# An even/odd split of the D-axis DFT, and gate/up weights loaded in small early pieces, in a fused spectral-mixer and gated-MLP kernel

## The chip, the cores and the metric

One core of one Trainium2 chip. The metric is device microseconds of one execution; lower is better. All executions quoted are "fast" (granted TensorE clock close to 1.0 unless said). Names used below: PE is TensorE, PEld its weight loads, DVE VectorE, ACT ScalarE, POOL GpSimd, SP the engine whose queue issues all DMAs. "Span" is the time between the first and the last instruction of the profiled execution; the device time is some 2 us longer.

## The reference, cut to what matters

```python
# x: (1, 2048, 640) bf16;  w_r, w_i: (2048, 321);  w_gate, w_up: (640, 1536);  w_down: (1536, 640)
def reference(x, w_r, w_i, B_x, w_gate, w_up, w_down):
    xn = _layernorm(x, axis=-1)
    X = rfft2(xn.astype(float32), axes=(-2, -1))          # S axis: 2048, D axis: 640
    y = irfft2(X * (w_r + 1j * w_i), s=(2048, 640), axes=(-2, -1)).astype(bfloat16)
    h = (xn @ w_gate) * (xn @ w_up)                        # no activation
    return x + y + h @ w_down
```

## The kernel before

All tensors live in one SBUF arena. The 2048 rows are worked in 16 blocks of 128. Each block goes through LayerNorm (DVE, POOL), a transpose T0 on PE (five 128x128 matmuls) into X^T, the D-axis DFT "D" (PE, against a cosine/sine table `fd`), its eviction, and the first part of the S-axis DFT "S128" (four 128x324 matmuls). After the last block come the middle stages (T1, S16, weight product, T2, S16i), in eleven groups, then the inverse transforms and the down projection. Independently of the spectral chain, 96 "GU" tiles (ten 128x256 matmuls each: gate and up of one 128-feature tile for 256 rows) need only X^T and the weights; each is evicted by ACT and multiplied on DVE or POOL.

The program writes tasks with assumed durations, priorities and dependences; a list scheduler in Python, run when the program is built, fixes the order of every engine's queue. On the chip each queue runs strictly in that order, with semaphore waits. GU tasks have a low priority: they fill PE where the plan finds a gap. "Filler" matmuls on zeros, and a "warm-up" of 56 such matmuls, occupy PE early on where the plan has nothing useful.

```python
# --- D stage of block b (cuts marked ...) ---
def em_t0(c, ...):
    for j in range(5):
        ins = c.e.transpose(psb[...], v_xn[:, sl, j * 128:(j + 1) * 128], v_sm[:, 0, :])
...
def em_d(c, b=b):                                  # 10 matmuls 128x324: 5 chunks of d, real and imaginary
    for j in range(5):
        for cc in range(2):
            ins = c.e.matmul(ps[:, bk + cc, 0:_LP], v_xt[:, j, b * 128:(b + 1) * 128],
                             v_fd[:, j, cc, :], start=(j == 0), stop=(j == 4))
def em_ed(c, ...):                                 # one ACT (or DVE) copy of 2 x 324
    return c.e.activation(v_a[:, ar, :, :], ps[:, bk:bk + 2, 0:_LP], _ACTF.Copy)
...
# --- gate/up weights: 8 slots; tiles 0-3 and 4-7 in two DMAs each of 640 KB, 8-11 later into freed slots ---
_NGW = 8
_FT_GROUPS = ((0, 1, 2, 3, 4, 5, 6, 7), (8, 9, 10, 11))
pl_ = 0.027 if q4 == 0 else 0.047                  # DMA priority; first S128 table has 0.025
...
# --- a GU tile ---
for w in range(2):
    for j in range(5):
        ins = c.e.matmul(ps[:, bk, w * 256:(w + 1) * 256], v_gw[:, w, j, r, :],
                         v_xt[:, j, c8 * 256:(c8 + 1) * 256], start=(j == 0), stop=(j == 4))
...
self.slack = {"pe": 1000.0, "act": 300.0, "dve": 400.0, "pool": 100.0, "sp": 0.0}   # of the planner
```

## Time and profile before

253.41 us, median of 5 runs (252.97 to 255.22); span 251.6 us, granted clock 1.000.

The page's first part gives the busy time of each engine, the second the busy tenths in 40 slices of the span (6.3 us each), the fourth the chain of work that ended last:

```profile
...
PE 244.7 (97%) x2286; PEld 202.2 (80%) x2286; DVE 153.9 (61%) x408; ACT 109.7 (44%) x194; POOL 24.3 (10%) x35
...
PE   8969999999999999999999999999999999999995
...
DVE  5868984208799999984722222222257767766654
...
PE 86%; DVE 5%; DMA 4%; SPq 1%; POOL 1%; issue 1%; ACT 1%
...
```

PE is busy nearly everywhere, and it is 86% of the chain. In windows (us from the start; busy us, with the number of instructions that ran in the window, wholly or in part; then clock and DMA):

```profile
...
core 0: us, PE busy (x) PEld busy (x) DVE busy (x) ACT busy (x) POOL busy (x), PEclk, DMA share, GB/s
...
15.00:60.00 45.00, 44.12 (x407) 34.08 (x405) 26.65 (x83) 25.02 (x40) 21.82 (x29) 1.00 0.52 168
60.00:123.00 63.00, 62.60 (x705) 56.31 (x703) 54.24 (x132) 36.30 (x56) 0.00 (x0) 1.00 0.15 52
123.00:178.00 55.00, 55.00 (x506) 49.11 (x504) 16.49 (x55) 30.12 (x51) 0.00 (x0) 1.00 0.14 31
178.00:240.00 62.00, 62.00 (x471) 45.92 (x470) 40.47 (x87) 12.74 (x36) 0.00 (x0) 1.00 0.23 65
...
```

From 60 us on PE has no gap worth naming (62.60 of 63, 55.00 of 55, 62.00 of 62). DVE is loaded in 15–123 us and less so later. "PE busy" includes the pipelined tail of each matmul and useless filler matmuls, so the page alone doesn't say how much of PE's time is work. The groups that the change touches (line, engine, operation, output and input, count; busy us, mean ns of one; idle time before):

```profile
...
L1019 PE MATMUL ps<-arena 128*128 128x256 bf16 x960 | 108.5, 273 | 2.2 <-DMA arena<-in_B_w_up_dram 2.0 <-ACT arena L1030 0.2
...
L821 PE MATMUL ps<-arena 128*128 128x324 bf16 x160 | 23.8, 300 | 0.4 <-DVE arena L808 0.4
...
L832 ACT ACTIVATE arena<-ps 128x648 bf16<-128x648 f32 x16 | 11.4, 710 | 11.3 <-PE ps L821 11.3
...
```

The mean of 300 ns for a D matmul is the length of its record, from its start to a modelled end. What it costs PE is the step from one start to the next, which the timeline gives (start, us, engine, line, count, idle time before and who ended it):

```profile
...
9.76 0.44 PE L796 MATMUL ps<-arena 128*128 128x128 bf16 x5
...
14.56 1.25 PE L1019 MATMUL ps<-arena 128*128 128x256 bf16 x10 [1.97 <-DMA arena<-in_B_w_up_dram]
...
40.19 2.94 PE L821 MATMUL ps<-arena 128*128 128x324 bf16 x20 [0.39 <-DVE arena L808]
42.97 0.30 PE L842 MATMUL ps<-arena 128*128 128x324 bf16 x1
...
43.52 0.72 PE L796 MATMUL ps<-arena 128*128 128x128 bf16 x10
44.08 0.30 PE L842 MATMUL ps<-arena 128*128 128x324 bf16 x1
...
44.63 2.93 PE L821 MATMUL ps<-arena 128*128 128x324 bf16 x20
...
```

L796 is T0, L821 D, L842 to L845 S128, L1019 GU. Twenty D matmuls, two blocks of them, take 40.19 to 42.97, which is 0.139 us each. The whole round of two blocks, from 40.19 to 44.63, is D, S128 and T0 without a GU tile between. The first GU tile starts at 14.56, after a wait of 1.97 us for the w_up weights.

### The profile page before, as it was taken

Reading aid. Unit: us, or ns where it says so; the run is one execution under the profiler, and the core shown is the slowest. Engines: PE = TensorE matmul, PEld = TensorE weight load, DVE = VectorE, ACT = ScalarE, POOL = GpSimd, SP = SyncE. Lnnn points to the kernel's source line nnn. Section 1 sums busy time; section 2 is a strip of 40 time slices with the busy share of each in tenths; the row PEclk is TensorE's granted clock in tenths of the full one; section 3 lists DMA queues with packets and bytes.
Section 4 is the critical chain, followed back from the end, with each engine's and each line's share of the span. In section 5 each row is a group of like instructions: output and inputs, shape, how many; then the busy total and the mean of one; then the engine's idle time right before and its main releaser. Section 6 shows DMA issues by size and latency. Waiting matters only on the chain.

```text
span 251.6 us, 5511 instructions
## 1 busy us (share of the span) xinstructions
PE 244.7 (97%) x2286; PEld 202.2 (80%) x2286; DVE 153.9 (61%) x408; ACT 109.7 (44%) x194; POOL 24.3 (10%) x35
## 2 busy tenths in 40 slices
PE   8969999999999999999999999999999999999995
PEld 8767766789999999898888888888777777777773
DVE  5868984208799999984722222222257767766654
ACT  2345555664554555557655555555213113113120
POOL 0066978000000000000000000000000000000000
PEclk9999999999999999999999999999999999999999
DMA  6997009328000000107202700000022132122121
GB/s 204 376 387 271 0 9 311 100 55 361 3 0 3 4 0 3 52 3 252 90 26 58 154 3 0 3 0 3 13 63 70 52 85 76 52 81 78 54 79 40
DMA packets 22505, 21.84 MB, mean 87 GB/s; under 512 B 6352, under 2 KB 21072, under 8 KB 22352
## 3 DMA queue, kind: packets, MB, share of 16 engines
q1 hardware_dynamic: 22480, 21.49, 27.4%
q8 instruction: 18, 0.29, 0.5%
q14 instruction: 7, 0.06, 0.1%
HBM read 18.86 MB, written 2.62 MB: 85 GB/s over the span
## 4 chain that ended last, share of the span: by engine, by line
PE 86%; DVE 5%; DMA 4%; SPq 1%; POOL 1%; issue 1%; ACT 1%
PE ps L1019 41%; PE ps L1152 21%; PE ps L821 4%; DMA arena<-in_B_w_up_dram 4%; PE ps L1112 3%; PE ps L1110 3%; PE ps L1067 2%; PE ps L940 2%; PE ps L961 2%; PE ps L884 2%; PE ps L905 2%; PE ps L1077 2%; SPq L647 1%; PE ps L796 1%; POOL arena L784 1%; DVE arena L808 1%
## 5 line engine op out<-in xcount | busy, mean ns | idle before, releaser
L1019 PE MATMUL ps<-arena 128*128 128x256 bf16 x960 | 108.5, 273 | 2.2 <-DMA arena<-in_B_w_up_dram 2.0
L1019 PEld LDWEIGHTS ps<-arena 128*128 128x128 bf16 x960 | 92.8, 98 | 13.4 <-issue 2.1
L1030 ACT ACTIVATE arena<-ps 128x512 bf16<-128x512 f32 x96 | 57.3, 597 | 49.4 <-PE ps L1019 48.8
L1037 DVE TENSOR_TENSOR arena<-arena 128x256 bf16<-128x256 bf16 x93 | 26.9, 289 | 48.4 <-ACT arena L1030 47.9
L1152 PE MATMUL ps<-arena 128*128 128x320 bf16 x384 | 54.6, 299 | 0.0
L1152 PEld LDWEIGHTS ps<-arena 128*128 128x128 bf16 x384 | 37.5, 98 | 13.9
L1121 ACT ACTIVATE arena<-ps 128x321 f32<-128x321 f32 x16 | 7.0, 439 | 52.8 <-PE ps L1112 52.7
L919 DVE TENSOR_TENSOR arena<-ps,arena 128x512 bf16<-128x512 f32 (+1 forms) x44 | 25.3, 636 | 0.0
L821 PE MATMUL ps<-arena 128*128 128x324 bf16 x160 | 23.8, 300 | 0.4 <-DVE arena L808 0.4
L1162 DVE TENSOR_TENSOR arena<-ps,arena 128x320 bf16<-128x320 f32 x32 | 15.6, 488 | 12.5 <-PE ps L1152 12.5
L821 PEld LDWEIGHTS ps<-arena 128*128 128x128 bf16 x160 | 15.2, 97 | 7.2 <-DVE arena L808 0.7
L832 ACT ACTIVATE arena<-ps 128x648 bf16<-128x648 f32 x16 | 11.4, 710 | 11.3 <-PE ps L821 11.3
L972 ACT ACTIVATE arena<-ps 128x1024 bf16<-128x1024 f32 x10 | 10.2, 1022 | 8.8 <-PE ps L961 8.8
L1140 DVE TENSOR_TENSOR arena<-arena 128x640 f32<-128x640 f32 x16 | 13.1, 821 | 1.1
L1112 PE MATMUL ps<-arena 128*128 128x319 bf16 x48 | 13.6, 300 | 0.0
L1110 PE MATMUL ps<-arena 128*128 128x321 bf16 x48 | 13.5, 299 | 0.0
L854 ACT ACTIVATE arena<-ps 128x648 bf16<-128x648 f32 x16 | 11.3, 708 | 4.7 <-PE ps L845 4.7
L773 POOL TENSOR_SCALAR arena<-arena 128x640 bf16<-128x640 bf16 x14 | 11.1, 799 | 14.8 <-DVE arena L718 14.8
L1088 DVE CAST arena<-ps 128x512 bf16<-128x512 f32 x11 | 7.6, 692 | 7.8 <-PE ps L1067 7.8
L808 DVE COPY arena<-ps 128x640 bf16<-128x640 bf16 x16 | 7.3, 480 | 8.0 <-PE ps L796 7.9
L784 POOL TENSOR_SCALAR arena<-arena 128x640 bf16<-128x640 bf16 x14 | 11.0, 796 | 2.2 <-DVE arena L762 1.9
L701 DVE BATCH_NORM_STATS2 arena<-arena 128x6 f32<-128x320 bf16 x16 | 7.6, 475 | 3.7 <-DMA arena<-in_A_x_dram 3.7
(65 smaller groups left out, 227.4 us busy)
## 6 DMA issues: line engine op xcount, KB each, us to landing
arena<-in_A_x_dram SPq DMA_DIRECT2D x18, 160.0 KB, 2.3
out_dram<-arena SPq DMA_DIRECT2D x32, 80.0 KB, 1.9
arena<-c_tinv SPq DMA_DIRECT2D x1, 2048.0 KB, 7.7
arena<-in_A_x_dram SPq DMA_DIRECT2D x3, 640.0 KB, 11.8
arena<-in_B_w_down_dram SPq DMA_DIRECT2D x1, 1920.0 KB, 7.9
arena<-c_t SPq DMA_DIRECT2D x4, 384.0 KB, 10.2
arena<-in_A_w_r_dram SPq DMA_DIRECT2D x1, 1284.0 KB, 7.7
arena<-in_A_w_i_dram SPq DMA_DIRECT2D x1, 1284.0 KB, 11.4
```

The costliest lines, as they stand in the source:

```text
L784: return c.e.tensor_scalar(v_xn[:, sl, :], v_xn[:, sl, :], v_rs[:, b:b + 1], 0.0, AluOpType.mult, AluOpType.add)
L821: ins = c.e.matmul(ps[:, bk + cc, 0:_LP], v_xt[:, j, b * 128:(b + 1) * 128], v_fd[:, j, cc, :], start=(j == 0), stop=(j == 4))
L832: return c.e.activation(dst, src, _ACTF.Copy)
L919: ins = c.e.tensor_tensor(dst, x5[:, :, cc, :, :], wv, AluOpType.mult)
L1019: ins = c.e.matmul(ps[:, bk, w * 256:(w + 1) * 256], v_gw[:, w, j, r, :], v_xt[:, j, c8 * 256:(c8 + 1) * 256], start=(j == 0), stop=(j == 4))
L1030: return c.e.activation(v_gbf[:, rr, :], ps[:, bk, :], _ACTF.Copy)
L1037: return c.e.tensor_tensor(v_ht[:, ft, c8 * 256:(c8 + 1) * 256], v_gbf[:, rr, 0:256], v_gbf[:, rr, 256:512], AluOpType.mult)
L1110: c.e.matmul(ps[:, bk, 0:321], v_z2[:, r3, lt, 0, :], v_g[:, lt, 0:321], start=(lt == 0), stop=(lt == 2))
L1112: ins = c.e.matmul(ps[:, bk + 1, 1:320], v_z2[:, r3, lt, 1, :], v_g[:, lt, 321:640], start=(lt == 0), stop=(lt == 2))
L1140: return c.e.tensor_tensor(v_yn[:, r2, :], v_yn[:, r2, :], v_xr[:, r2, :], AluOpType.add)
L1152: ins = c.e.matmul(ps[:, bk, 0:320], v_ht[:, ft, sa * 128:(sa + 1) * 128], v_wd[:, ft, hf * 320:(hf + 1) * 320], start=(ft == 0), stop=(ft ...
L1162: return c.e.tensor_tensor(v_out[:, r2, sl3], ps[:, bk, 0:320], v_yn[:, r2, sl3], AluOpType.add)
```

## The change

Intent: the cosine of frequency 320 - l at row d is (-1)^d times that of frequency l, and the sine is -(-1)^d times it. So the sums over even d, E(l), and over odd d, O(l), for l = 0 to 160 give all 321 frequencies: X(l) = E(l) + O(l), and X(320 - l) has the real part E - O and the imaginary part O - E. Each half needs 162 columns instead of 324, so D takes 6 matmuls of 324 columns instead of 10 (the d rows are permuted by strided T0 reads into even and odd chunks; the chunk that holds both enters both sums). The price is in the eviction: E + O, E - O and O - E have to be formed, with mirrored writes. Because X^T is now permuted, the gate/up weight rows must be loaded in the same permutation. These loads are also split into 30 DMAs of 128 KB, get 12 resident slots, and the first ten are put ahead of the first S128 table.

```diff
-_NGW = 8
+_NGW = 12
+_DT = ((0, 2), (256, 2), (512, 1), (1, 2), (257, 2))
...
-                    for j in range(5):
-                        for cc in range(2):
-                            ins = c.e.matmul(ps[:, bk + cc, 0:_LP], v_xt[:, j, b * 128:(b + 1) * 128],
-                                             v_fd[:, j, cc, :], start=(j == 0), stop=(j == 4))
+                    for q in range(6):
+                        tj = (0, 1, 2, 2, 3, 4)[q]
+                        ins = c.e.matmul(ps[:, bk + q // 3, 0:324], v_xt[:, tj, b * 128:(b + 1) * 128],
+                                         v_fd[:, q, :], start=(q % 3 == 0), stop=(q % 3 == 2))
...
+                def em_eo(c, td=td, ar=ar):                      # O: PSUM -> SBUF, f32, 324 elements (ACT)
+                    ...
+                    return c.e.activation(v_osb[:, ar, :, :], src, _ACTF.Copy)
                 def em_ed(c, td=td, ar=ar):
-                    src = ps[:, bk:bk + 2, 0:_LP]
-                    ...return c.e.activation(dst, src, _ACTF.Copy)
+                    e3 = ps[:, bk, 0:324].rearrange("p (c l) -> p c l", c=2)
+                    c.e.tensor_tensor(v_a[:, ar, :, 0:161], e3[:, :, 0:161], v_osb[:, ar, :, 0:161], AluOpType.add)
+                    c.e.tensor_tensor(v_a[:, ar, 0, 320:160:-1], e3[:, 0, 0:160], v_osb[:, ar, 0, 0:160],
+                                      AluOpType.subtract)
+                    return c.e.tensor_tensor(v_a[:, ar, 1, 320:160:-1], v_osb[:, ar, 1, 0:160], e3[:, 1, 0:160],
+                                             AluOpType.subtract)
...
-                    pl_ = 0.027 if q4 == 0 else 0.047
+                    if ftp == 0:
+                        pl_ = opts.get("pgw0", 0.022) if q4 == 0 else opts.get("pgw1", 0.032)
+                    else:
+                        pl_ = opts.get("pgw2", 0.07)
+                    for w_, src_ in ((0, B_w_gate), (1, B_w_up)):
+                        for j in range(5):
+                            s0, st = _DT[j]
+                            ...
+                            dma("ld_gw%d_%d_%d" % (f0, w_, j), dst_, src_[s0:s0 + 128 * st:st, fs], 128 * 1024, ...)
```

More of the change, by code (lines that the diff above doesn't have):

```diff
@@ L389, in _bf16_bits, with _dperm @@
     return r.astype(np.uint16)
+_DT = ((0, 2), (256, 2), (512, 1), (1, 2), (257, 2))
+def _dperm():
+    return [np.arange(128, dtype=np.int64) * st + s0 for (s0, st) in _DT]
 def _build_tables():
@@ L415, in _build_tables @@
     t["sm"] = _bf16_bits(sm)
-    d = np.arange(_D, dtype=np.int64)[:, None]
-    l = np.arange(_LP, dtype=np.int64)[None, :]
-    ang = two_pi * ((d * l) % _D).astype(np.float64) / _D
-    valid = (np.arange(_LP) <= 320).astype(np.float64)[None, :]
-    fd = np.zeros((_D, 2, _LP), np.float64)
-    fd[:, 0, :] = np.cos(ang) * valid
-    fd[:, 1, :] = -np.sin(ang) * valid
-    t["fd"] = _bf16_bits(fd.reshape(5, 128, 2, _LP).transpose(1, 0, 2, 3))
+    dmap = _dperm()
+    lv = np.arange(162, dtype=np.int64)[None, :]
+    lval = (np.arange(162) <= 160).astype(np.float64)[None, :]
+    fd = np.zeros((128, 6, 2, 162), np.float64)
+    for q, (tj, par) in enumerate(((0, 0), (1, 0), (2, 0), (2, 1), (3, 1), (4, 1))):
+        dd = dmap[tj][:, None]
+        ang = two_pi * ((dd * lv) % _D).astype(np.float64) / _D
+        sel = ((dmap[tj] % 2) == par).astype(np.float64)[:, None] * lval
+        fd[:, q, 0, :] = np.cos(ang) * sel
+        fd[:, q, 1, :] = -np.sin(ang) * sel
+    t["fd"] = _bf16_bits(fd)
     s1 = np.arange(128, dtype=np.int64)[:, None]
@@ L530, in _build @@
         b_gw = alloc("GW", _NGW * 2 * 5 * 128)
+        b_gwj = [[sch.buf("GW_%d_%d" % (w_, j_), lay["GW"][0] + (w_ * 5 + j_) * _NGW * 128, _NGW * 128)
+                  for j_ in range(5)] for w_ in range(2)]
         b_gbf = alloc("GBF", 3 * 512)
@@ L542, in _build @@
         b_dum = alloc("DUM", 256)
+        b_osb = alloc("OSB", 2 * 648)
         total = cur[0]
@@ L553, in _build @@
         o_at = lay["AT"][0]
-        b_fd = alloc("FD", 5 * 2 * _LP, at=o_at)
-        b_t128 = alloc("T128", 16 * 3 * 128, at=o_at + 5 * 2 * _LP)
+        b_fd = alloc("FD", 6 * 2 * 162, at=o_at)
+        b_t128 = alloc("T128", 16 * 3 * 128, at=o_at + 6 * 2 * 162)
         b_tinv = alloc("TINV", 16 * 2 * 256, at=o_at)
@@ L597, in _build @@
         v_xn = V("XN").rearrange("p (r d) -> p r d", r=_NSLOT_XN)
-        v_fd = V("FD").rearrange("p (j c l) -> p j c l", j=5, c=2)
+        v_fd = V("FD").rearrange("p (q n) -> p q n", q=6)
         v_t128 = V("T128").rearrange("p (s m k) -> p s m k", s=16, m=3)
@@ L602, in _build @@
         v_a = V("A").rearrange("p (r c l) -> p r c l", r=2, c=2)
+        v_osb = V("OSB").bitcast(_F32).rearrange("p (r c l) -> p r c l", r=2, c=2)
         v_yeo = V("YEO").bitcast(_F32).rearrange("p (r n) -> p r n", r=2)
@@ L651, in _build @@
         ld_sm = dma("ld_sm", v_sm, d_sm, 128 * 768, [(b_sm, None)], prio=0.005)
-        ld_fd = dma("ld_fd", v_fd, d_fd, 128 * 6480, [(b_fd, None)], prio=0.015)
+        ld_fd = dma("ld_fd", V("FD"), d_fd.rearrange("p q c l -> p (q c l)"), 128 * 6 * 648, [(b_fd, None)],
+                    prio=0.015)
         ld_t = []
@@ L684, in _build, with em_apad @@
               bank="pair", cls="warm", selffree=True)
+        def em_apad(c):
+            return c.e.memset(v_a[:, :, :, _NL:_LP], 0.0)
+        T("a_pad", ("dve",), 80.0, em_apad, writes=[(b_a, ("pad", 0, 1))], prio=0.5)
         def em_wpad(c):
@@ L795, in em_t0 @@
                     for j in range(5):
+                        s0, st = _DT[j]
                         ins = c.e.transpose(psb[:, bk * 1024 + j * 128: bk * 1024 + (j + 1) * 128],
-                                            v_xn[:, sl, j * 128:(j + 1) * 128], v_sm[:, 0, :])
+                                            v_xn[:, sl, s0:s0 + 128 * st:st], v_sm[:, 0, :])
                     return ins
@@ L823, in em_d @@
                     return ins
-                td = T("D_%d" % b, "pe", 10 * _d_pe_mm(_LP), em_d,
+                td = T("D_%d" % b, "pe", 6 * _d_pe_mm(324), em_d,
                        reads=[(b_xt, ("s", b * 128, (b + 1) * 128)), (b_fd, None)], prio=pb, bank="pair", cls="a")
+                def em_eo(c, td=td, ar=ar):
+                    bk = bank_of(td)
+                    src = ps[:, bk + 1, 0:324].rearrange("p (c l) -> p c l", c=2)
+                    if c.e is nc.scalar:
+                        return c.e.activation(v_osb[:, ar, :, :], src, _ACTF.Copy)
+                    return c.e.tensor_copy(v_osb[:, ar, :, :], src)
@@ L827, in em_ed @@
+                eo = T("eO_%d" % b, _EV32, {"dve": _d_dve_psum(324), "act": _d_act(324)}, em_eo,
+                       writes=[(b_osb, ("r", ar, ar + 1))], prio=pb - 0.001, after=[td])
+                td.deps |= set(d for d in eo.deps if d is not td)
                 def em_ed(c, td=td, ar=ar):
                     bk = bank_of(td)
-                    src = ps[:, bk:bk + 2, 0:_LP]
-                    dst = v_a[:, ar, :, :]
-                    if c.e is nc.scalar:
-                        return c.e.activation(dst, src, _ACTF.Copy)
@@ L833, in em_ed @@
-                    return c.e.tensor_copy(dst, src)
-                ed = T("eD_%d" % b, _EV32, {"dve": _d_dve_psum(2 * _LP), "act": _d_act(2 * _LP)}, em_ed,
-                       writes=[(b_a, ("r", ar, ar + 1))], prio=pb - 0.001, frees=td)
-                td.deps |= set(d for d in ed.deps if d is not td)
+                    e3 = ps[:, bk, 0:324].rearrange("p (c l) -> p c l", c=2)
+                    c.e.tensor_tensor(v_a[:, ar, :, 0:161], e3[:, :, 0:161], v_osb[:, ar, :, 0:161], AluOpType.add)
@@ new lines, in em_ed @@
+                    c.e.tensor_tensor(v_a[:, ar, 0, 320:160:-1], e3[:, 0, 0:160], v_osb[:, ar, 0, 0:160],
+                                      AluOpType.subtract)
+                    return c.e.tensor_tensor(v_a[:, ar, 1, 320:160:-1], v_osb[:, ar, 1, 0:160], e3[:, 1, 0:160],
+                                             AluOpType.subtract)
+                ed = T("eD_%d" % b, "dve", _d_dve_psum(322) + 2 * _d_dve_psum(160), em_ed,
+                       reads=[(b_osb, ("r", ar, ar + 1))], writes=[(b_a, ("r", ar, ar + 1))], prio=pb - 0.001,
+                       frees=td)
@@ L838, in em_s @@
+                td.deps |= set(d for d in ed.deps if d is not td and d is not eo)
                 def em_s(c, b=b, ar=ar):
@@ L983, in _build @@
         for ftp, ftg in enumerate(_FT_GROUPS):
-            if ftp == 0 and opts.get("gw_chunk", 4) == 4:
+            if True:
                 for q4 in range(len(ftg) // 4):
@@ L988, in _build @@
                     fs = slice(f0 * 128, (f0 + 4) * 128)
-                    pl_ = 0.027 if q4 == 0 else 0.047
-                    for w_, src_ in ((0, wgv), (1, wuv)):
-                        dst_ = v_gw[:, w_, :, r0:r0 + 4, :].rearrange("p j r f -> p j (r f)")
-                        dma("ld_gw%d_%d" % (f0, w_), dst_, src_[:, :, fs], 640 * 1024,
-                            [(b_gw, ("r", 8 * w_ + r0, 8 * w_ + r0 + 4))], prio=pl_ + 0.0001 * w_,
-                            semkey=("gw", r0, w_))
+                    if ftp == 0:
[4 more added lines that the diff above has]
+                        for j in range(5):
+                            s0, st = _DT[j]
+                            dst_ = v_gw[:, w_, j, r0:r0 + 4, :].rearrange("p r f -> p (r f)")
+                            dma("ld_gw%d_%d_%d" % (f0, w_, j), dst_, src_[s0:s0 + 128 * st:st, fs], 128 * 1024,
+                                [(b_gwj[w_][j], ("r", r0, r0 + 4))], prio=pl_ + 0.0001 * w_ + 0.00001 * j,
+                                semkey=("gw", r0, w_))
             else:
@@ L1002, in _build @@
                         pl_ = 30.0 + 0.5 * ft
-                    for w_, src_ in ((0, wgv), (1, wuv)):
-                        dma("ld_gw%d_%d" % (ft, w_), v_gw[:, w_, :, r0, :], src_[:, :, fs], 640 * 256,
-                            [(b_gw, ("r", 8 * w_ + r0, 8 * w_ + r0 + 1))], prio=pl_ + 0.0001 * w_,
-                            semkey=("gw2", r0, w_))
+                    for w_, src_ in ((0, B_w_gate), (1, B_w_up)):
+                        for j in range(5):
+                            s0, st = _DT[j]
+                            dma("ld_gw%d_%d_%d" % (ft, w_, j), v_gw[:, w_, j, r0, :],
+                                src_[s0:s0 + 128 * st:st, fs], 128 * 256,
+                                [(b_gwj[w_][j], ("r", r0, r0 + 1))],
+                                prio=pl_ + 0.0001 * w_ + 0.00001 * j, semkey=("gw2", r0, w_))
             for c8 in range(8):
@@ L1022, in _build @@
                     gu = T("GU_%d_%d" % (ft, c8), "pe", 10 * _d_pe_mm(256), em_gu,
-                           reads=[(b_gw, ("r", r, r + 1)), (b_gw, ("r", 8 + r, 8 + r + 1)),
+                           reads=[(b_gwj[w_][j_], ("r", r, r + 1)) for w_ in range(2) for j_ in range(5)] + [
                                   (b_xt, ("s", c8 * 256, (c8 + 1) * 256))],
```

## The prediction

> **What bounds the kernel now.** The page gives PE 97% busy, the chain 86% PE, granted clock 1.000. From 55 us on PE never waits: the windows view shows it busy 55.76 of 56.0 us in 55–111, 55.00 of 55.0 in 123–178, 70.97 of 71.0 in 178–249. Steps between matmuls, from the timeline: 0.109 us for gate/up (128x256), 0.139 for the D-axis DFT (128x324; ten in 1.39 us). At such steps all useful matmuls add up to about 235 of the 251.6 us span. The rest is the tail after PE's last matmul (2.6 us), start-up before the first gate/up matmul at 14.56 us (3.9 us of it useful; the rest warm-up, fillers and a 1.97 us wait for the w_up DMA), and small gaps. Between 26 and 52 us PE runs only T0, D and S128, nearly without gaps: 4.4 us per two blocks, 2.77 of them D. So D is on the bound.
>
> **What changes.**
> 1. D falls from 10 to 6 matmuls per block: 64 x 0.139 = 8.9 us less PE work. The Trainium skill ("TensorE: Matmul & The Clock Gate", Back-to-back issue gap) gives N/2.4 + 2.5 ns, 137.5 for 324; the trace's 139 agrees.
> 2. D's eviction, one ACT copy of 648 elements (710 ns), becomes one ACT copy of 324 (about 440, like the 128x321 copy) and three VectorE operations: 322 elements (about 490, like FIN 128x320) and twice 160 (about 310, between the 128x64 at 214 and the 128x512 at 678). That is 1.1 us per block, 15–18 us more DVE work in the first 55 us, where DVE is now busy 34. The chain from D to S128 lengthens from 0.7 to about 1.7 us.
> 3. Gate/up weights come in 30 DMAs of 128 KB, the first ten ahead of the first S128 table; fd shrinks. Before the first gate/up matmul 2.5 MB must land instead of 3.2: about 2 us earlier, though ten issues at 0.47 us use most of that rate up. The tiles 8–11 lose their 256-byte rows; their reload was hidden, so that gains nothing.
>
> **How much lies on the path.** After 55 us all is PE-bound, with gate/up work left until 178 us, so PE time saved early is filled with gate/up matmuls and comes off the end almost 1:1, if PE is kept fed before 55 us. Ideal: 251.6 - 8.9 - 2 = 240.7 span, 242.5 us time. Against it: the first phase turns DVE-bound (about 50 us of DVE work, plus gate/up products, in some 52 us); queues run in a fixed planned order, and the plan takes the eviction for 0.86 us where I expect 1.1. So PE will wait 2–4 us in 15–58 us. The tail stays.
>
> **Predicted: 244.8 us, range 241 to 249.5.** Faster by over 2%: 0.80; within 2%: 0.18; slower: 0.02.
>
> **What would show it.** 96 D matmuls at the same step; first gate/up matmul at 11–13 us; DVE over 85% busy in 15–55 us, about 168–172 us in total; gate/up matmuls in 26–52 us, where there are none now; new PE waits on DVE (S128 on the butterfly, T0 on LayerNorm), 2–4 us; later phases unchanged in shape; ACT total down about 4 us.
>
> **What would make it wrong.** Faster: the order absorbs the DVE work and PE hardly waits. Slower: the butterfly runs longer than estimated (reversed writes, or waiting for POOL's LayerNorm operations: the tiny tensor_tensor takes 0.7 us beside POOL at 30–38 us), so the D stage ends well after 58 us with PE waiting; or the 128 KB issues delay the x tiles.

## The result, and the profile after

243.98 us, median of 9 runs (243.59 to 245.7), against 253.43 us for the kernel before, median of 16. The ratio is 0.9635, with a 95% interval of 0.9613 to 0.9656. Ratios here and below divide the mean time of one kernel's fast runs by that of the other's of the same rounds on the same chip, so they are not quite the ratio of the quoted medians. The profiled run has a span of 242.9 us and a clock of 1.000.

The page of the kernel after, the lines that answer to those of before:

```profile
...
PE 237.6 (98%) x2242; PEld 198.5 (82%) x2242; DVE 162.1 (67%) x454; ACT 107.5 (44%) x197; POOL 24.3 (10%) x35
...
PE   8989999999999999999999999999999999999995
...
DVE  5877998864579999999737222222377677667654
...
PE 88%; SPq 6%; DMA 3%; DVE 1%; issue 1%; ACT 0%
...
```

The windows of the kernel after:

```profile
...
15.00:60.00 45.00, 44.70 (x406) 36.29 (x404) 36.74 (x136) 29.50 (x55) 23.09 (x30) 1.00 0.54 173
60.00:123.00 63.00, 62.76 (x727) 57.22 (x726) 53.84 (x129) 34.45 (x51) 0.00 (x0) 1.00 0.15 46
...
178.00:240.00 62.00, 62.00 (x470) 45.77 (x467) 41.52 (x91) 12.64 (x36) 0.00 (x0) 1.00 0.24 69
...
```

In 15–60 us DVE went from 26.65 to 36.74 us busy, while PE is as full as before (44.70 us against 44.12). The groups of the kernel after:

```profile
...
L1059 PE MATMUL ps<-arena 128*128 128x256 bf16 x960 | 110.5, 273 | 0.2 <-ACT arena L1070 0.2
...
L841 PE MATMUL ps<-arena 128*128 128x324 bf16 x96 | 15.6, 300 | 0.0
...
L860 DVE TENSOR_TENSOR arena<-ps,arena 128x322 bf16<-128x322 f32 x16 | 7.8, 484 | 3.5 <-ACT arena L851 3.5
...
L851 ACT ACTIVATE arena<-ps 128x324 f32<-128x324 f32 x16 | 7.0, 440 | 3.5 <-PE ps L841 2.4
...
L861 DVE TENSOR_TENSOR arena<-ps,arena 128x160 bf16<-128x160 f32 x16 | 5.1, 316 | 0.0
...
L863 DVE TENSOR_TENSOR arena<-arena,ps 128x160 bf16<-128x160 f32 x16 | 5.0, 312 | 0.0
...
```

D has 96 matmuls instead of 160. The three butterfly operations take 484 + 316 + 312 ns, 1.11 us a block. The PE timeline of the kernel after (L816 is T0, L841 D, L874 to L877 S128, L1059 GU):

```profile
...
12.35 0.44 PE L816 MATMUL ps<-arena 128*128 128x128 bf16 x5
13.72 0.31 PE L874 MATMUL ps<-arena 128*128 128x324 bf16 x1 [0.92 <-DMA arena<-c_t]
...
15.56 2.35 PE L1059 MATMUL ps<-arena 128*128 128x256 bf16 x20
...
42.69 1.26 PE L1059 MATMUL ps<-arena 128*128 128x256 bf16 x10
43.78 0.99 PE L841 MATMUL ps<-arena 128*128 128x324 bf16 x6
44.61 0.30 PE L874 MATMUL ps<-arena 128*128 128x324 bf16 x1
...
45.16 0.99 PE L841 MATMUL ps<-arena 128*128 128x324 bf16 x6
46.00 1.25 PE L1059 MATMUL ps<-arena 128*128 128x256 bf16 x10
...
```

Two things stand out. GU tiles now stand between the D matmuls (42.69, 46.00). And the first GU tile begins at 15.56 us, an S128 having waited 0.92 us for its table: later than before, not earlier.

An account of PE's time makes this exact. Add up, over the whole timeline of PE, the step from each start to the next, by kind of matmul; a wait is then counted with the matmul before it. Totals in us, from the first matmul (1.05 us in both):

```
                           before    after   difference
D                           22.18    13.32     -8.86
warm-up and fillers         10.96    10.63     -0.33
T0                           4.99     5.55     +0.56   (0.92 of after is the wait for the S128 table)
S128                         9.40     8.85     -0.55
GU                         104.88   105.38     +0.50
all other matmuls           95.51    95.45     -0.06
sum                        247.92   239.18     -8.74
```

The span fell by 8.7 us (251.6 to 242.9), the D steps by 8.86. Apart from that, PE's time hardly changed in sum. The tail is the same: the span less 1.05 us less the sum leaves 2.6 us in both.

One part of this sum is chance. The 56 warm-up matmuls, which the change doesn't touch, took 5.78 us in this execution of after and 4.57 in that of before. In both they start about every 107 ns at first and about every 56 ns later, but the slow steps number 52 in after and 28 in before. Over the twelve profiles with 56 warm-up matmuls they took 4.40 to 5.95 us. So 1.2 us of the difference between two profiles at the start need not come from the change, and the profiled run of after (244.8 us) is slower than its median: the two later profiles of the same kernel have spans of 241.9 and 241.6 us.

Yet the D stage itself did not become shorter: the last S128 matmul starts at 53.9 us before and at 60.4 us after. It became longer by 6.5 us while the kernel became shorter by 8.7. In 15–60 us 87 GU matmuls ran before and 190 after.

### The profile page after: what moved, and what is told of

It is laid out like the page before. It is cut to its first block, busy times and chain, and to the rows that moved or that the text cites. A ratio compares the mean times of both kernels' runs of the same rounds, so it can differ in the third digit from the quotient of the medians.

```text
span 242.9 us, 5472 instructions
## 1 busy us (share of the span) xinstructions
PE 237.6 (98%) x2242; PEld 198.5 (82%) x2242; DVE 162.1 (67%) x454; ACT 107.5 (44%) x197; POOL 24.3 (10%) x35
## 4 chain that ended last, share of the span: by engine, by line
PE 88%; SPq 6%; DMA 3%; DVE 1%; issue 1%; ACT 0%
PE ps L1059 41%; PE ps L1192 21%; SPq L661 6%; PE ps L841 4%; DMA arena<-in_A_x_dram 3%; PE ps L1152 3%; PE ps L1150 3%; PE ps L1107 3%; PE ps L972 2%; PE ps L993 2%; PE ps L937 2%; PE ps L916 2%; PE ps L1117 2%; PE ps L816 1%; PE ps L874 1%; PE ps L875 1%
## 5 line engine op out<-in xcount | busy, mean ns | idle before, releaser
L1059 PE MATMUL ps<-arena 128*128 128x256 bf16 x960 | 110.5, 273 | 0.2 <-ACT arena L1070 0.2
L1059 PEld LDWEIGHTS ps<-arena 128*128 128x128 bf16 x960 | 92.7, 98 | 11.7 <-ACT arena L1070 0.4
L1192 PEld LDWEIGHTS ps<-arena 128*128 128x128 bf16 x384 | 37.5, 98 | 13.9
L841 PE MATMUL ps<-arena 128*128 128x324 bf16 x96 | 15.6, 300 | 0.0
L886 ACT ACTIVATE arena<-ps 128x648 bf16<-128x648 f32 x16 | 11.4, 710 | 5.5 <-PE ps L877 5.0
L841 PEld LDWEIGHTS ps<-arena 128*128 128x128 bf16 x96 | 9.2, 97 | 3.6
L860 DVE TENSOR_TENSOR arena<-ps,arena 128x322 bf16<-128x322 f32 x16 | 7.8, 484 | 3.5 <-ACT arena L851 3.5
L1172 DVE TENSOR_TENSOR arena<-arena 128x319 f32<-128x319 f32 x16 | 7.7, 482 | 3.2 <-ACT arena L1162 3.2
L1107 PE MATMUL ps<-arena 128*128 128x256 bf16 x64 | 9.6, 272 | 0.0
```

The source lines that it names most:

```text
L841: ins = c.e.matmul(ps[:, bk + q // 3, 0:324], v_xt[:, tj, b * 128:(b + 1) * 128], v_fd[:, q, :], start=(q % 3 == 0), stop=(q % 3 == 2))
L1107: ins = c.e.matmul(ps[:, bk, lt * 256:(lt + 1) * 256], v_z1[:, sa, cc, 128 * lt:128 * lt + 128], v_tinv[:, sa, cc, :], start=(cc == 0), st ...
L1192: ins = c.e.matmul(ps[:, bk, 0:320], v_ht[:, ft, sa * 128:(sa + 1) * 128], v_wd[:, ft, hf * 320:(hf + 1) * 320], start=(ft == 0), stop=(ft ...
```

## The experiments

Theory A: PE is the bound from 15 us to the end, so the D matmuls removed come off one for one, and GU tiles use the PE time that the slower eviction leaves open. Rivals: B, that the new loads bring part of the gain and the butterfly takes as much back; C, that DVE is now at its limit and PE has time to spare before 60 us; E, that the D stage simply became shorter.

### dft_only and loads_only: each half of the change alone

```diff
# dft_only, against after: loads as before
-_NGW = 12
+_NGW = 8
-   pl_ = opts.get("pgw0", 0.022) ...          # ten DMAs of 128 KB per four tiles, all early
+   pl_ = 0.027 if q4 == 0 else 0.047          # three DMAs per matrix and chunk (rows are permuted), tiles 8-11 late
# loads_only, against before: D stage untouched
-_NGW = 8
+_NGW = 12
+_DT = ((0, 1), (128, 1), (256, 1), (384, 1), (512, 1))   # then the load loop of after
```

> The change with the even/odd D stage alone: gate/up weights ordered, sized and reloaded as before (8 slots, first chunk behind the first S128 table, tiles 8-11 in small DMAs late; each load in three DMAs instead of one because the rows are permuted). Theory A (the gain is the 64 D matmuls taken off PE, the loads add nothing): 243.5 to 244.8 us, as the whole change. Theory B (the early, resident weights bring the roughly 2 us that I predicted, and the DVE butterfly takes about as much back): 245.5 to 247 us.

> The kernel before with the new weight loads alone (12 slots, 30 DMAs of 128 KB, first ten ahead of the first S128 table), D stage untouched. Theory A: 253 to 254.2 us, the same as before within 0.3%. Theory B: 251 to 252 us. Either way the first gate/up matmul should come earlier than 14.56 us.

Measured on one chip, with the kernel before at 253.57 us: dft_only 245.03 us (244.88 to 245.2), ratio 0.9656 (0.9628 to 0.9685); loads_only 251.93 us (251.84 to 252.24), ratio 0.9930 (0.9901 to 0.9959).

So the even/odd DFT alone brings 8.5 us of the gain. Its 245.03 us lies between the ranges of A (to 244.8) and B (from 245.5); its ratio is that of the whole change, as A has it. But the loads alone are worth 1.6 us on the old DFT, 0.4 to 1% by the ratio's interval, where A expected nothing; there B was right. On top of the DFT what they add is not resolved: the whole change had ratios of 0.9635, 0.9652 and 0.9669 in three sets of runs, dft_only 0.9656 in one. The gain of the loads doesn't come the way I had thought either. In loads_only the first GU tile starts at 15.04 us, later than the 14.56 of before, where it had been expected earlier: the 1.97 us wait for w_up is gone, but S128 now waits 1.85 us for its table. By the account of PE's steps, warm-up, fillers, T0 and S128 together shrank by 1.2 us (25.35 to 24.14); of this the fillers, 56 instead of 66, and the wait counted with them are 1.1 us, and T0 is 0.5. What set these free was not tested.

### mm_pad: put the PE time back

```diff
+                    for q in (0, 1, 2, 3):      # overwritten by the real matmuls that follow
+                        c.e.matmul(ps[:, bk + q // 2, 0:324], v_xt[:, q, b * 128:(b + 1) * 128],
+                                   v_fd[:, q, :], start=True, stop=True)
                     for q in range(6):
```

> The changed kernel with four useless 128x324 matmuls put back in front of each D stage (overwritten by the real ones), all queue orders unchanged. Theory A (PE time counts one for one): 64 x 0.139 = 8.9 us more, 252.5 to 253.3 us, about the time before. Rival C (in 15-60 us DVE is the limit and PE has spare time there): less than 4 us more, below 248 us.

Measured: 252.3 us (251.77 to 252.72), ratio 0.9936 (0.9892 to 0.9979). That is about 8 us above the changed kernel's medians (243.98, 244.13 and 244.38 in three other sets of runs), or 6.8 to 7.6 us by the ratios. In its trace the useless matmuls occupy 8.88 us of PE. Most of that comes back, if not quite all that A expected (252.5 us or more). The queues were not replanned, and DVE's work was as heavy as in after. Rival C (less than 4 us) fails: PE has at most 1 to 2 us to spare before 60 us.

### bfly_plus1 and bfly_x2: how much slack DVE has

Each butterfly operation's copy writes to a place that is unused at that time. The order of all queues is the same as in after.

```diff
# bfly_plus1: the third operation twice;  bfly_x2: all three twice
+                    d3_ = v_ht[:, b, 1506:1666] if b < 12 else v_ht[:, b - 4, 1666:1826]
+                    c.e.tensor_tensor(d3_, v_osb[:, ar, 1, 0:160], e3[:, 1, 0:160], AluOpType.subtract)
```

> The changed kernel with the third butterfly operation done twice (the copy goes to an unused place), all queue orders unchanged: 16 x about 0.23 us = 3.7 us more DVE work in 9-59 us. Theory A (DVE has slack behind the gate/up matmuls): 0 to 1.5 us more. Rival C (DVE is at the limit): about 3.7 us more, 247.5 us.

> The changed kernel with all three butterfly operations done twice (copies to an unused place), all queue orders unchanged: 16 x about 0.87 us = 14 us more DVE work before 60 us, where DVE had about 6 us of idle time in 15-55 us. Theory D (DVE has a slack of some 6 us behind the gate/up matmuls, and is the limit beyond it): 6 to 10 us more, 250 to 254 us, PE waiting on DVE for about that long in 15-70 us. If DVE does not matter at all: below 245.5 us.

Measured: bfly_plus1 245.03 us, ratio 0.9655 (0.9620 to 0.9691), not told apart from the changed kernel (0.9635 to 0.9669 in three sets; the interval leaves room for about 1 us). bfly_x2 250.95 us (250.49 to 251.85), ratio 0.9916, against 244.13 us and 0.9652 of the control after_again on the same chip: 6.8 us more for some 14 us of added DVE work. The waits of PE in bfly_x2 (who, on whom; us in total, times, longest; L881 is S128, L870 the butterfly, L753 and L771 LayerNorm on DVE):

```profile
...
PE ps L881 <- DVE arena L870: 2.0, 5, 0.6
...
PE ps L881 <- DVE arena L753: 1.4, 2, 0.9
...
PE ps L881 <- DVE arena L771: 0.9, 1, 0.9
...
```

These lines make 4.3 of the 6.8 us; a wait of 1.1 us for the S128 table also stands there. In the kernel after, the one PE wait on DVE in this stage was 0.3 us:

```profile
...
PE ps L874 <- DVE arena L863: 0.3, 1, 0.3
...
```

So DVE had room for the butterfly (about 14 us) and for some 4 us more, and not for 14 more. Since 14 us cost 6.8, some 7 us of DVE time was free; this is worked out, not measured by itself.

### after_again: the control of those runs

> The changed kernel itself once more, as the control of this chip session: 243.6 to 244.8 us, ratio to the kernel before 0.961 to 0.966 if the sessions agree.

Measured: 244.13 us (243.27 to 245.41), ratio 0.9652 (0.9624 to 0.9679).

### nofill_before and nofill_after: no GU tiles during the D stage

```diff
-                           prio=pu, bank="single", cls="glu")
+                           prio=pu, bank="single", cls="glu", after=[t_evS128[15]])
```

> The kernel before, gate/up matmuls allowed only after the last S128 eviction. It ran 7 of them before 55 us (7.6 us of PE), so 4 to 8 us more: 257 to 261 us.

> The changed kernel, gate/up matmuls allowed only after the last S128 eviction. Theory A/D (the D stage itself became DVE-bound and no shorter; the gain exists only because gate/up matmuls fill the PE time set free): D stage ends at 53 to 58 us with PE idle a third of it, 258 to 265 us, so the change is worth nothing or is a loss against nofill_before. Rival E (the D stage simply became shorter by its PE saving): 8 to 9 us below nofill_before.

Measured: nofill_before 261.06 us (260.04 to 261.61), ratio 1.0307; nofill_after 265.01 us (264.05 to 267.27), ratio 1.0480. Without the GU tiles the same change makes the kernel about 4 us slower. Windows of nofill_after (the last columns are the granted clock, the DMA share and GB/s):

```profile
...
core 0: us, PE busy (x) PEld busy (x) DVE busy (x) ACT busy (x) POOL busy (x), PEclk, DMA share, GB/s
...
20.00:26.00 6.00, 3.88 (x28) 1.98 (x25) 5.74 (x23) 2.40 (x5) 1.71 (x4) 1.00 1.03 377
26.00:34.00 8.00, 5.95 (x36) 4.07 (x36) 6.55 (x21) 1.59 (x3) 4.74 (x7) 0.57 0.36 125
34.00:41.00 7.00, 4.57 (x34) 2.55 (x32) 6.93 (x23) 3.82 (x7) 4.89 (x7) 0.96 0.00 0
41.00:46.00 5.00, 5.00 (x35) 3.27 (x35) 4.04 (x15) 1.89 (x4) 1.39 (x2) 0.72 0.95 261
...
```

DVE is busy 5.74 of 6, 6.55 of 8 and 6.93 of 7 us in the first three, and PE waits: 4.6 us in all for the butterfly and 3.8 us for POOL's LayerNorm operations. Moreover the clock falls to 0.57 and 0.72 in two of the windows: twelve D matmuls from 29.29 to 32.51 us take 0.268 us each instead of 0.139 (L816 is T0, L841 D):

```profile
...
27.98 1.50 PE L816 MATMUL ps<-arena 128*128 128x128 bf16 x10 [3.04 <-POOL arena L803]
29.29 3.44 PE L841 MATMUL ps<-arena 128*128 128x324 bf16 x12
32.51 1.23 PE L816 MATMUL ps<-arena 128*128 128x128 bf16 x10
...
```

The Trainium skill ("TensorE: Matmul & The Clock Gate", What's actually happening) says that the array's clock is halved after an idle window of about 3.4 us. In the halving this trace agrees: 0.268 is about twice 0.139. In the idle time it doesn't: the granted clock is 0.50 from 26.73 us on, when PE had stood idle for 1.8 us of the 3.04 us wait that ended at 27.98, and again from 40.39 us on, after waits of 1.55 and 0.47 us. As an estimate, busy time times the missing clock in these windows (5.95 x 0.43 + 4.57 x 0.04 + 5.00 x 0.28) is about 4 us. So the loss against nofill_before is of the size of the lost clock; without it the change would be worth about nothing. No run held the clock up, but the four executions of nofill_after fit this: spans of 261.9, 261.9, 263.7 and 265.1 us at mean clocks of 0.987, 0.987, 0.981 and 0.974, so that span times clock is 258 to 259 us in each, and nofill_before has 258.8 at 1.000. Rival E (8 to 9 us faster without filling) fails.

### The start: ln1_first, start_table, start_gw, after_again2

These look into one of the two steps of the prediction that clearly failed, the early first GU tile (the other is the PE wait of 2–4 us).

```diff
# ln1_first: block 0's butterfly behind block 1's LayerNorm on DVE
-   ... writes=[(b_a, ("r", ar, ar + 1))], prio=pb - 0.001,
+   ... writes=[(b_a, ("r", ar, ar + 1))], prio=pb - 0.001 + (0.21 if b == 0 else 0.0),
# start_table: that, and
-   nwarm = opts.get("nwarm", 14)               # 56 warm-up matmuls
+   nwarm = opts.get("nwarm", 10)               # 40 (and their planned time 3800 instead of 5200 ns)
-   pl_ = opts.get("pgw0", 0.022)
+   pl_ = opts.get("pgw0", 0.027)               # behind the first S128 table (0.025)
# start_gw: ln1_first, 40 warm-up matmuls, loads as in after, and
-   sch.dma_bw = float(opts.get("dma_bw", 330.0))
+   sch.dma_bw = float(opts.get("dma_bw", 290.0))
```

> The changed kernel with one priority changed: the butterfly of block 0 behind the LayerNorm of block 1 on DVE; replanned. If the late first gate/up matmul (15.56 us instead of my 11 to 13) comes from that order, T0 of block 1 starts near 10.5 us instead of 12.35 and the first gate/up matmul at 13 to 14.5 us, and 0.5 to 1.5 us come off: 242.5 to 243.6. If the weights' landing holds it, no change, with a PE wait on the weight DMAs.

> As ln1_first, and the first S128 table loaded ahead of the gate/up weights, and 40 instead of 56 warm-up matmuls. If the wait for the table (0.92 us in the profile of after) counts: no PE wait on the table, first gate/up matmul at 12.5 to 13.5 us, 242 to 243.2 us; if the weights, now 0.4 MB later, hold PE instead: a PE wait on the w_up DMA of about 1 us and no gain over ln1_first.

> As ln1_first with 40 warm-up matmuls, loads as in after, and a slower DMA rate in the plan, so that the first gate/up tile is planned ahead of S128 of block 0 and that one's wait for its table is covered. First gate/up matmul at 12 to 13 us, no PE wait on the table, 241.8 to 243 us, the best of the three if the table's landing was the hold-up.

> The changed kernel unaltered, as the control on the chip of these runs: 243.6 to 244.8 us.

Measured on one chip, the kernel before at 252.92 us:

```
                 median us   lowest    highest   ratio     first GU tile   PE wait for the S128 table
after_again2      244.38     243.36    246.23    0.9669      14.74 us        0.7 us
ln1_first         243.97     243.51    246.42    0.9668      14.22 us        1.4 us
start_table       242.93     242.81    243.10    0.9601      13.10 us        none
start_gw          244.53     243.38    244.66    0.9654      12.64 us        none
```

In ln1_first T0 of block 1 moved from 11.74 (after_again2) to 10.07 us, as expected, but PE then stood longer before the table of S128, and the 0.5 to 1.5 us expected did not come off:

```profile
...
10.07 0.44 PE L816 MATMUL ps<-arena 128*128 128x128 bf16 x5
...
11.24 0.99 PE L841 MATMUL ps<-arena 128*128 128x324 bf16 x6
13.66 0.31 PE L874 MATMUL ps<-arena 128*128 128x324 bf16 x1 [1.42 <-DMA arena<-c_t]
...
14.22 2.35 PE L1059 MATMUL ps<-arena 128*128 128x256 bf16 x20
...
```

With the table ahead of the weights too, and 16 warm-up matmuls fewer, there is no wait (start_table):

```profile
...
10.99 0.44 PE L816 MATMUL ps<-arena 128*128 128x128 bf16 x5
...
11.72 0.30 PE L874 MATMUL ps<-arena 128*128 128x324 bf16 x1
...
12.27 0.99 PE L841 MATMUL ps<-arena 128*128 128x324 bf16 x6
13.10 2.34 PE L1059 MATMUL ps<-arena 128*128 128x256 bf16 x20
...
```

So neither the DVE order nor the table alone held the start; removing the first only moved the wait to the second. In none of these runs did PE wait for the weights themselves. start_table is the fastest kernel, 1.4 us below its control by the medians, and its 4 runs all lie below the 6 of the control. The size is uncertain: three of the six control runs took 245.09 to 246.23 us, two of them at a mean clock of 0.993, and against the other three (243.36 to 243.66) the gain is some 0.6 us. How much of it is the table's and how much the shorter warm-up's was not tested. start_gw began GU earliest and gained nothing, where it had been expected to be the best: its first GU tile came 0.5 us before start_table's, but it ran 50 pairs of fillers against 43, and PE waited 0.6 us on a butterfly once. The first GU start is thus a poor measure of the start; the PE time that goes to useless matmuls and waits is the better one.

## Why the prediction was right or wrong

The time (244.8 predicted, 243.98 measured) and the direction were right. The steps:

- **PE is the bound, D is on it, 8.9 us come off: right.** D steps fell by 8.86 us, the span by 8.7; the DFT alone gave 8.5 us; putting the matmuls back cost 7 to 8.
- **The freed PE time is filled with GU tiles: right, and it is the condition for the gain.** With GU tiles shut out of the D stage, the change lost 4 us instead of gaining 9.4; by the estimate above the lost clock makes up these 4, so that without GU tiles the change is worth about nothing.
- **The cost of the eviction, 1.1 us a block and 15–18 us of DVE: right per operation** (484, 316 and 312 ns for the estimates 490, 310, 310), but the total of 168–172 us on the page was too high: 162.1, 8.2 more than before. I added mean durations to a busy time in which overlaps are counted once. From start to start the three operations take 0.40, 0.23 and 0.23 us, 0.86 a block, about 14 us in all; three T0 evictions (1.4 us) moved from DVE to ACT; and some small LayerNorm operations took about 2.6 us less in sum. The butterfly did not wait for POOL, which I had feared. The Trainium skill ("SBUF — State Buffer", Who interferes with whom) says that DVE contends with a POOL operation that reads SBUF only where it has two SBUF inputs (or a 2-port mode). The trace of after agrees: beside POOL's LayerNorm the butterfly with one PSUM input kept its 0.48 us (at 34.28 and 35.91), while the 4-element tensor_tensor with two SBUF inputs took 0.64 us at 35.35, against 0.15 at 26.06 with POOL idle.
- **"So PE will wait 2–4 us in 15–58 us": wrong; 0.3 us.** The term was mis-sized because the plan put GU tiles where S128 would have waited. bfly_plus1 shows that even 4 us more DVE work costs at most about 1 us; only bfly_x2 produced the waits that I had forecast (4.3 us).
- **"About 2 us earlier" for the first GU tile: wrong in the profile after; 15.56 us, later than the 14.56 before** (14.54 and 14.74 in the two repeats, about as before). The slower warm-up of that execution (1.2 us, chance) makes up the lateness against before, but not the miss of 11–13. I took the landing of the weights for the limit, and by that the step fails: the order of the queues was the limit. T0 of block 1 stood behind 28 pairs of fillers and behind a LayerNorm that itself stood behind block 0's butterfly, and S128 waited for the table that the change had moved behind the weights (0.92 and 0.7 us in two profiles, not at all in the third). dft_only, with the old loads, started GU at 14.09 us, earlier than any profile of the whole change.
- These two terms, 2 us of gain and 2–4 us of loss, were both wrong with opposite signs. That they nearly cancel is luck, and part of why the total came out so near; without the two, 251.6 - 8.9 gives 242.7 span, and 242.9 was measured (241.9 and 241.6 in the repeats).
- **The D stage ends at about 58 us: nearly right**; its last S128 started at 60.4 us. **It turns DVE-bound: not borne out.** DVE was 84% busy in 14.4–55 us, where I had said over 85, but with 3.9 us more DVE work in bfly_plus1 the stage ended no later (last S128 at 60.0 us). Only without GU tiles (nofill_after) did DVE hold PE up for long. **The tail and the later stages unchanged: right.** ACT fell by 2.2 us instead of 4, because of the three T0 evictions.

## What to carry to other kernels

A stage's own length says little about a change where a low-priority pool of work can fill its gaps: this stage grew by 6.5 us and the kernel shrank by 8.7. Count instead what the bounding engine must still do, from start-to-start steps, and check that the pool lasts and that the plan will really place it there. When a kernel starts with a chain of loads and a fixed order, removing one hold-up may only uncover the next, so look for what PE does in that time (useless matmuls, waits) and not for when one stage begins.

## What the Trainium skill lacked or had wrong

- "TensorE: Matmul & The Clock Gate", Back-to-back issue gap: it says that in real streams of weight load and matmul the step is about 81 ns at N = 128, and that N/2.4 + 2.5 ns holds for isolated matmuls only. Here every matmul has its own weight load (in after 81 loads for the 81 matmuls of S16, and 81 for the 81 transposes T2), and the steps are 56 ns at 128 columns (4.5 us for either 81), 109 at 256 and 139 at 324. The formula for the isolated one fits all three; the 81 ns does not.
- "VectorE: DVE Perf Modes", in the section on the TRN2 errata, gives (N + 151)/0.96 ns for an fp32 tensor_tensor add: 493 ns for 322 elements, 324 for 160. It was checked there at 512 and 2048 elements. With one operand in PSUM and a bf16 result 484 and 312 to 316 ns were measured, within 4%; mirrored writes cost nothing extra (in bfly_x2 316 and 313 ns, the same two operations with plain writes 314 and 311).
- "TensorE: Matmul & The Clock Gate", What's actually happening: in nofill_after the clock was halved when PE had been idle for 1.8 us on end, and not for the 3.4 us of the page.
